# Transnormer attention with an RWKV channel mix on one core: the last tile's two parts stored by one DMA each, one middle tile's stores cut in four

## The chip, the core and the metric

The kernel runs on one core of one Trainium2 chip. The metric is device time in microseconds (us) of one execution. Before the change the median of three runs is 197.99 us (197.79 to 198.03).

The core has five engines that work side by side: TensorE (PE, matrix products into the PSUM memory; PEld is its loading of weights), VectorE (DVE), ScalarE (ACT), GpSimd (POOL) and SyncE (SP). Data moves between the chip's main memory (DRAM) and the on-chip memory SBUF (128 partitions) by DMA. A DMA is issued by an instruction on an engine's queue (here SP, ACT or POOL), carried out by some of the core's 16 DMA engines in packets, and reported by a semaphore.

## The reference

The attention part multiplies, for each of 8 batches and 8 heads, q by k-transposed-times-v, normalises each row of 64, and scales it. The channel mix then mixes each token with the one before it, and gates one product by another:

```python
kv = np.einsum('bhsd,bhse->bhde', k, v)
out = np.einsum('bhsd,bhde->bhse', q, kv)
out = out / np.sqrt(np.mean(out * out, axis=-1, keepdims=True) + 1e-06) * g_norm
x = out.transpose(0, 2, 1, 3).reshape(B, S, H * D)            # 8 x 576 x 512
xk = mu_k * x + (1.0 - mu_k) * x_prev                         # x_prev: one token earlier
xr = mu_r * x + (1.0 - mu_r) * x_prev
k = np.maximum(xk @ w_k, 0.0)                                 # 512 -> 1024
v = k * k @ w_v                                               # 1024 -> 512
r = 1.0 / (1.0 + np.exp(-(xr @ w_r)))
return r * v                                                  # 8 x 576 x 512, float32
```

## The kernel before

**Tiles.** A batch has 576 tokens. They are dealt out as 9 groups j of 64 rows: token number is p times 9 plus j, with p from 0 to 63. Two batches are taken together, which makes 18 groups of 64, or 9 tiles of two groups: a tile t fills the 128 partitions, group 2t in partitions 0 to 63 and group 2t + 1 in partitions 64 to 127. A tile is named by its batch and number, (7, 8) being the last.

**Order.** `ORDER`, at the head of the kernel, is a list of words written by hand; each word is one step, and each engine carries out its instructions in the order in which the words emit them. The words that matter here:

- `R.b.t`: the gate of a tile, four matrix products (L665) and a sigmoid on ScalarE (L668) into a tile `sig`.
- `V.b.t.part`: the product with `w_v`, eight matrix products (L675) into a PSUM tile of 128 by 512.
- `fin.b.t`: `finish`. VectorE multiplies the PSUM tile by `sig` into an SBUF tile `out` (L688), float32, 128 by 512, and two stores follow on SyncE's queue, one for each half of the partitions.
- `fip.b.t` and `sta.b.t`: the same in two words, the first half's store on SyncE's queue, the second half's later on ScalarE's.
- `L.0` and `L.1`: the last tile (7, 8), computed by `last_vv` in two parts of its columns: the wide part, columns 0 to 383, and then the narrow one, 384 to 511. Each part has eight matrix products (L683), one multiplication (L688) and two stores, the first half's on SyncE's queue and the second half's on ScalarE's.

The end of `ORDER` is

```
... fin.6.3 fin.7.4 R.7.8=1 V.7.5.0=5 V.7.5.1 fip.7.7 fip.7.5 sta.7.7 sta.7.5 L.0=3 L.1=0
```

and the tile (4, 3), which the change names, is finished at the end of the seventh of the list's eight periods, after (5, 4) and before (6, 2):

```
... fin.5.4 ... V.4.3.1 ks.6.5' fin.4.3          (next period:)  ... V.6.2.1 fin.6.2 ...
```

**Stores.** `store` (L698 is its `dma_start`) writes one half of a tile: 64 partitions of `out` go to 64 rows of the result. In DRAM, rows of one group lie 9 rows of 512 floats apart; the two groups of a tile are neighbours, one row apart, as long as they lie in one batch. The groups of the last tile are 7 and 8 of batch 7.

**Tiles' room.** `out` tiles take one of seven buffers in turn; a buffer is given back when the second half's store is emitted (`leave`), and the next multiplication into it waits until its stores have landed.

**The end.** When the last word has been emitted, the closing code (L836 in the profile) has SyncE wait for every semaphore that is still open, and a barrier of all engines follows.

The tiles' names in the profile, with a number: `out__3425` is tile (4, 3), `out__3527` tile (6, 2), `out__3698` tile (7, 5), `out__3712` the wide part of the last tile, `out__3725` its narrow part.

Of the kernel before, what the change touches and what calls it, by code (L numbers as in the profile page):

```python
# [117 lines left out]
def kernel(  # L118
# [13 lines left out]
    nc = tc.nc  # L132

    B, H, S, HD = q.shape
    C = H * HD
# [3 lines left out]
    G = 9  # L139
# [43 lines left out]
    for w, mu in enumerate((moe_mu_k, moe_mu_r)):  # L183
        nc.sync.dma_start(out=rows[4 * w:4 * w + 4, :], in_=mu.rearrange("(j p) -> j p", p=128))
    nc.sync.dma_start(out=rows[8:9, :].rearrange("o (e p) -> o e p", e=2),
                      in_=g_norm.rearrange("(o p) -> o p", o=1).unsqueeze(1).to_broadcast([1, 2, HD]))
# [58 lines left out]
    def take(key, shape, dtype, name):  # L245

        n = chosen.pop(0) if chosen else idle[0]
        idle.remove(n)
        held[key] = n, bank(n, shape, dtype, name)
        return held[key][1]  # L250

    def give(key):
        n, ps = held.pop(key)
        idle.append(n)
        return ps
# [13 lines left out]
    def half(i):  # L269
        return slice(64 * i, 64 * i + 64)  # L270
# [376 lines left out]
    def slot(kind, key, shape, dtype):  # L647

        n = place[kind, key] = free[kind].pop(0)
        return work.tile(shape, dtype, tag=f"{kind}{n}_", name=f"{kind}{n}_", bufs=1)  # L650

    def leave(kind, key):
        free[kind].append(place.pop((kind, key)))
# [24 lines left out]
    def last_vv(b, t, part):  # L678

        c = (slice(0, 3 * C // 4), slice(3 * C // 4, C))[part]  # L680
        ps = take(("last", part), [128, c.stop - c.start], FP32, "ps_v")
        for fc in range(NFC):
            nc.tensor.matmul(ps, sqk[:, fc, 128 * t:128 * t + 128], wv_sb[:, fc, c], start=(fc == 0), stop=(fc == NFC - 1))  # L683
        finish(b, t, ("last", part), c, (nc.sync, nc.scalar))

    def finish(b, t, key, c=slice(0, C), queues=(nc.sync, nc.sync)):
        o = outs[b, t, c.start] = slot("out", (b, t, c.start), [128, c.stop - c.start], FP32)
        DVE.tensor_mul(out=o, in0=give(key), in1=sig[b, t][:, c])  # L688
        for i, q_ in enumerate(queues):
            store(b, t, i, q_, c)  # L690
        if c.stop - c.start == C:
            leave("sig", (b, t))

    outs = {}

    def store(b, t, i, q_, c=slice(0, C)):
        bb, j = b - b % 2 + (2 * t + i) // G, (2 * t + i) % G
        q_.dma_start(out=out[bb].rearrange("(p j) c -> j p c", j=G)[j, :, c], in_=outs[b, t, c.start][half(i), :])  # L698
        if i == 1:
            leave("out", (b, t, c.start))  # L700

# [3 lines left out]
    for what in "wk.0.2 wk.1.2 k.0.2 q.0.2 v.0.2 wv.0.2 k.1.2 q.1.2 v.1.2 wv.2.4 wv.3.4 wr.0.1".split():  # L705
        name, i, n = what.split(".")
# [29 lines left out]
    def part_square(b, j, f0, f1, eng):  # L736
# [36 lines left out]
        "V": lambda eng, b, t, part: vv(b, t, part),  # L773
        "Vq": lambda eng, b, t, part: vv(b, t, part, 2),
        "fin": lambda eng, b, t: finish(b, t, ("v", b, t)),
        "fip": lambda eng, b, t: finish(b, t, ("v", b, t), queues=(nc.sync,)),
        "sta": lambda eng, b, t: store(b, t, 1, nc.scalar),
        "L": lambda eng, part: last_vv(B - 1, 8, part),
        "tab": lambda eng: ACT.preload_act_table_set("sigmoid_and_others"),  # L779
        "cast": lambda eng, n: evac(eng, x_in["kv"[n], 0][:, A], raw[:, n]),  # L780
# [60 lines left out]
```

## Time and profile before

| | |
|---|---|
| median of three runs | 197.99 us |
| the profiled execution | 198.81 us |
| its span, first to last instruction | 197.0 us |
| PE busy | 187.9 us, 95% of the span, mean granted clock 0.996 |
| DVE, ACT, POOL busy | 160.2, 135.3 and 28.2 us |
| DMA moved | 32.75 MB in 42958 packets |
| read and written in DRAM | 33.56 and 9.44 MB |

The profile belongs to one execution. Its span runs from the first instruction to the last; 1.81 us of that execution's time lie around it. An engine's busy time says how much of the span it worked. Instructions that issue a DMA are not counted as busy; they are listed for the queues SPq, ACTq and POOLq with the time that the issue took. What a DMA does after that is told by the DMA engines' share of busy time, by the bytes moved, by the count of packets, and by the time from issue to landing.

### The profile page before, as it was taken

Reading aid. Unit: us, or ns where it says so; the run is one execution under the profiler, and the core shown is the slowest. Engines: PE = TensorE matmul, PEld = TensorE weight load, DVE = VectorE, ACT = ScalarE, POOL = GpSimd, SP = SyncE. Lnnn points to the kernel's source line nnn. Section 1 sums busy time; section 2 is a strip of 40 time slices with the busy share of each in tenths; the row PEclk is TensorE's granted clock in tenths of the full one; section 3 lists DMA queues with packets and bytes.
Section 4 is the critical chain, followed back from the end, with each engine's and each line's share of the span. In section 5 each row is a group of like instructions: output and inputs, shape, how many; then the busy total and the mean of one; then the engine's idle time right before and its main releaser. Section 6 shows DMA issues by size and latency. Waiting matters only on the chain.

```text
span 197.0 us, 5692 instructions
## 1 busy us (share of the span) xinstructions
PE 187.9 (95%) x2343; PEld 110.3 (56%) x2343; DVE 160.2 (81%) x355; ACT 135.3 (69%) x273; POOL 28.2 (14%) x50
## 2 busy tenths in 40 slices
PE   7698999999999997999999999999999999999991
PEld 2345665465554774566744666765446666655441
DVE  1479899999999997999989999899998678465341
ACT  3494876765876995899594869998892867435520
POOL 7753334010023003200020040000000000000000
PEclk9999999999999999999999999999999999999998
DMA  5999999999999999999979889977526313125185
GB/s 216 215 211 206 194 207 209 206 207 241 257 200 149 216 265 128 221 230 246 200 121 173 163 149 245 229 104 104 142 53 118 86 43 77 25 57 131 40 210 152
DMA packets 42958, 32.75 MB, mean 166 GB/s; under 512 B 23852, under 2 KB 37428, under 8 KB 42932
## 3 DMA queue, kind: packets, MB, share of 16 engines
q0 software_dynamic: 14400, 16.19, 49.6%
q1 hardware_dynamic: 28132, 15.67, 36.7%
q10 hardware_dynamic: 400, 0.52, 0.9%
q8 instruction: 18, 0.29, 0.6%
q14 instruction: 8, 0.07, 0.1%
HBM read 33.56 MB, written 9.44 MB: 218 GB/s over the span
## 4 chain that ended last, share of the span: by engine, by line
PE 63%; DMA 24%; DVE 5%; POOL 2%; ACT 2%; issue 2%; DVEq 0%; POOLq 0%
PE ps_v L675 25%; PE ps_km L633 20%; PE ps_r L665 12%; DMA in_q<-in_q_dram 8%; DMA sq<-in_k_dram 7%; DMA qT__1367<-in_q 5%; DMA q<-in_q_dram 3%; PE ps_kv L287 2%; PE ps_u L317 1%; DVE yd L400 1%; PE ps_x L437 1%; DVE xr L620 1%; PE ps_v L683 1%; ACT L779 1%; DVE ss__2775 L362 1%
## 5 line engine op out<-in xcount | busy, mean ns | idle before, releaser
L675 PE MATMUL ps_v<-wv_sb,sqk 128*128 128x512 bf16 x280 | 66.6, 379 | 0.0
L633 PEld LDWEIGHTS <-wk_sb 128*128 128x128 bf16 x480 | 45.7, 98 | 17.0
L675 PEld LDWEIGHTS <-sqk 128*128 128x128 bf16 x280 | 26.6, 98 | 28.3 <-issue 0.2
L665 PE MATMUL ps_r<-wr_sb,xr 128*128 128x512 bf16 x144 | 34.8, 379 | 0.1
L665 PEld LDWEIGHTS <-xr 128*128 128x128 bf16 x144 | 14.0, 98 | 14.4 <-issue 0.3
L625 ACT ACTIVATE rt<-ps_km 128x320 bf16<-128x320 f32 (+2 forms) x17 | 7.9, 496 | 5.3 <-PE ps_km L633 3.5
L260 PE MATMUL ps_warm<-zeros 128*128 128x512 bf16 x28 | 9.2, 441 | 1.2 <-DVE eps L223 1.2
L633 PE MATMUL ps_km<-xk__880,wk_sb 128*128 128x192 bf16 (+1 forms) x64 | 9.2, 287 | 0.0
L633 PE MATMUL ps_km<-xk__3387,wk_sb 128*128 128x288 bf16 x64 | 9.0, 286 | 0.0
L633 PE MATMUL ps_km<-xk__2408,wk_sb 128*128 128x288 bf16 x64 | 8.7, 286 | 0.0
L633 PE MATMUL ps_km<-xk__1965,wk_sb 128*128 128x288 bf16 x64 | 8.7, 286 | 0.0
L633 PE MATMUL ps_km<-xk__2742,wk_sb 128*128 128x288 bf16 x64 | 8.7, 286 | 0.0
L633 PE MATMUL ps_km<-xk__3233,wk_sb 128*128 128x288 bf16 x64 | 8.7, 286 | 0.0
L633 PE MATMUL ps_km<-xk__1507,wk_sb 128*128 128x288 bf16 x64 | 8.3, 286 | 0.0
L427 ACT ACTIVATE xT<-ps_x,cols 128x256 bf16<-128x256 bf16 (+3 forms) x9 | 5.2, 588 | 3.6 <-PE ps_x L437 3.5
L260 PEld LDWEIGHTS <-zeros 128*128 128x128 bf16 x28 | 2.9, 109 | 5.0 <-issue 2.4
L724 PE MATMUL ps_km<-xk__371,wk_sb 128*128 128x320 bf16 x32 | 5.1, 300 | 0.5 <-DMA wk_sb<-in_moe_w_k_dram 0.5
L195 POOL DMA_DIRECT2D in_v<-in_v_dram x3 | 2.2, 747 | 19.7 <-PE ps_kv L287 17.2
L641 DVE TENSOR_TENSOR sqk<-rt 128x768 bf16<-128x768 bf16 (+3 forms) x7 | 4.9, 703 | 0.1
L427 ACT ACTIVATE xT<-xT,cols 128x1152 bf16<-128x1152 bf16 x4 | 5.0, 1294 | 0.0
L603 ACT ACTIVATE m__2401<-dx__2391,cols 128x576 bf16<-128x576 bf16 x4 | 2.9, 768 | 3.1 <-DVE dx__2391 L597 3.1
L688 DVE TENSOR_TENSOR out__3637<-ps_v,sig__3631 128x512 f32<-128x512 f32 x1 | 0.7, 691 | 5.3 <-ACT sig__3631 L668 5.3
(417 smaller groups left out, 372.7 us busy)
## 6 DMA issues: line engine op xcount, KB each, us to landing
q<-in_q_dram POOLq DMA_DIRECT2D x3, 576.0 KB, 14.7
sq<-in_k_dram POOLq DMA_DIRECT2D x3, 576.0 KB, 14.5
qT<-in_v_dram POOLq DMA_DIRECT2D x3, 576.0 KB, 11.4
in_v<-in_v_dram POOLq DMA_DIRECT2D x3, 576.0 KB, 14.7
in_q<-in_q_dram POOLq DMA_DIRECT2D x3, 576.0 KB, 10.2
in_k<-in_k_dram POOLq DMA_DIRECT2D x3, 576.0 KB, 17.0
wk_sb<-in_moe_w_k_dram POOLq DMA_DIRECT2D x2, 512.0 KB, 10.0
sqk<-in_k_dram SPq DMA_DIRECT2D x1, 576.0 KB, 3.7
```

The lines of the kernel that those rows point to most:

```text
L195: nc.gpsimd.dma_start(out=x_in[name, b], in_=by_token(dram[name], b))
L260: nc.tensor.matmul(ps, zeros[:, :128], zeros, start=True, stop=True)
L287: nc.tensor.matmul(ps[e][half(i), M, :], kb[half(e), 2 * M + i, tok(j)], vb[half(e), 2 * M + i, tok(j)], start=(j == 0), stop=(j == G - 1))
L317: nc.tensor.matmul(out_, qT_[half(r), b // 2, half(ct % 2)], kv_[half(r), 0 if r == i else 1, ct, :], start=True, stop=True)
L427: eng.activation(out=dst, in_=src, func=AF.Copy, scale=g_sb)
L603: eng.activation(out=out_, in_=in_, func=AF.Copy, scale=mu)
L625: eng.activation(out=dst, in_=ps, func=AF.Relu)
L633: nc.tensor.matmul(ps[:, n, :], wk_sb[:, cc, 128 * fc:128 * fc + 128], at[b]["xk"][:, cc, c0:c1], start=(cc == 0), stop=(cc == NHP - 1))
L641: eng.tensor_mul(out=sqk[:, fcs, o:o + n], in0=src, in1=src)
L665: nc.tensor.matmul(ps, xr[:, cc, 128 * t:128 * t + 128], wr_sb[:, cc, :], start=(cc == 0), stop=(cc == NHP - 1))
L675: nc.tensor.matmul(ps, sqk[:, fc, 128 * t:128 * t + 128], wv_sb[:, fc, :], start=(fc == 0), stop=(fc == NFC - 1))
L724: nc.tensor.matmul(ps[:, n, :], wk_sb[:, cc, 128 * fc:128 * fc + 128], at[0]["xk"][:, cc, c0:c1], start=(cc == 0), stop=(cc == NHP - 1))
```

## The change

`last_vv` no longer has `finish` store its parts. It issues one DMA for each part, over all 128 partitions: the wide part's on ScalarE's queue, the narrow part's on SyncE's. The DMA's DRAM side has three dimensions: 2 groups, 64 rows, the part's columns. Its SBUF side has two: 128 partitions, the part's columns. In the last tile two DMAs stand in place of four.

`finish` treats the tile (4, 3) apart: each of its two stores is cut into two halves of the columns, on the same queue, so that four DMAs of 64 rows and 256 columns stand in place of two of 64 rows and 512 columns. The address of a half's rows moves from `store` into a function of its own, `rows_of`.

```diff
@@ last_vv
-        finish(b, t, ("last", part), c, (nc.sync, nc.scalar))
+        finish(b, t, ("last", part), c, ())
+        (nc.scalar, nc.sync)[part].dma_start(
+            out=out[b].rearrange("(p j) c -> j p c", j=G)[2 * t - G:2 * t - G + 2, :, c], in_=outs[b, t, c.start])

@@ finish
         for i, q_ in enumerate(queues):
-            store(b, t, i, q_, c)
+            if (b, t) == (4, 3):
+                for c_ in (slice(0, C // 2), slice(C // 2, C)):
+                    q_.dma_start(out=rows_of(b, t, i)[:, c_], in_=outs[b, t, c.start][half(i), c_])
+                if i == 1:
+                    leave("out", (b, t, c.start))
+            else:
+                store(b, t, i, q_, c)

+    def rows_of(b, t, i):
+        bb, j = b - b % 2 + (2 * t + i) // G, (2 * t + i) % G
+        return out[bb].rearrange("(p j) c -> j p c", j=G)[j]
+
     def store(b, t, i, q_, c=slice(0, C)):
-        bb, j = b - b % 2 + (2 * t + i) // G, (2 * t + i) % G
-        q_.dma_start(out=out[bb].rearrange("(p j) c -> j p c", j=G)[j, :, c], in_=outs[b, t, c.start][half(i), :])
+        q_.dma_start(out=rows_of(b, t, i)[:, c], in_=outs[b, t, c.start][half(i), :])
```

## The prediction

> **What bounds the kernel now.** I read the engines' busy times first (PE 187.9 us of a span of 197.0, 95%), then the chain of waits, which says what ended last, then the instructions of the last microseconds in order of time, and last the DMA engines' share over short windows. The chain's last pieces (start, length, what):
>
> ```profile
> 189.61 1.73 PE ps_v L675 x8
> 191.34 1.31 PE ps_v L683 x8
> 192.66 0.04 DVEq L688
> 192.69 0.04 issue
> 192.74 0.06 DVE out__3712 L688
> ```
>
> PE never rests until 193.09, so whatever the change does before that is worth nothing unless it holds up PE. What remains is a tail of 3.9 us, from 193.1 to 197.0. The last instructions in order of time (start, length, queue, what):
>
> ```profile
> 192.74 0.56 DVE L688 TENSOR_TENSOR out__3712<-ps_v,sig__3684 128x384 f32<-128x384 f32 x1 [0.67 <-PE ps_v L683]
> 193.21 0.28 DVE L688 TENSOR_TENSOR out__3725<-ps_v,sig__3684 128x128 f32<-128x128 f32 x1
> 193.32 0.47 SPq L698 DMA_DIRECT2D out_dram<-out__3712  x1
> 193.32 0.50 ACTq L698 DMA_DIRECT2D out_dram<-out__3712  x1
> 193.88 0.55 SPq L698 DMA_DIRECT2D out_dram<-out__3725  x1
> 193.92 0.79 ACTq L698 DMA_DIRECT2D out_dram<-out__3725  x1
> ```
>
> The reader is to see that the narrow part is ready at 193.49 but its stores start only at 193.88 and 193.92, because each queue is still issuing its wide store. The DMA list gives 2.2 us from issue to landing for the last one, so it lands at 193.92 + 2.2 = 196.1, and the closing barrier takes the other 0.9 us. Now the DMA engines over short windows (window, its length, four columns of engine work, clock, then the DMA share and GB/s):
>
> ```profile
> 176.94:177.18 0.24, 0.24 (x3) 0.10 (x1) 0.24 (x1) 0.24 (x2) 0.00 (x0) 1.00 0.07 26
> ...
> 194.37:194.44 0.07, 0.00 (x0) 0.00 (x0) 0.00 (x0) 0.00 (x0) 0.00 (x0) 1.00 0.00 0
> 194.46:194.86 0.40, 0.00 (x0) 0.00 (x0) 0.00 (x0) 0.00 (x0) 0.00 (x0) 1.00 0.94 204
> 194.98:195.12 0.14, 0.00 (x0) 0.00 (x0) 0.00 (x0) 0.00 (x0) 0.00 (x0) 1.00 1.02 362
> ...
> 195.68:197.00 1.32, 0.00 (x0) 0.00 (x0) 0.00 (x0) 0.00 (x0) 0.00 (x0) 0.50 0.00 0
> ```
>
> Three things. The engines rest at 194.37 to 194.44 and start on the wide store at 194.46: 1.14 us after its issue, 0.09 us after the stores before it have ended. Then they are busy until 195.68, so the last two stores' bytes take **1.22 us**, and another 1.32 us pass between the last byte and the end of the span. And the first line is a single engine (a share of 0.07 is one of sixteen) that had fallen behind on a store: alone, it moves **26 GB/s**.
>
> **How many engines a DMA uses.** This decides the case. Each engine that takes part ends its share with one small packet, so the count of small packets tells how many took part. The DMA view of three windows, on SyncE's queue: one around the second load of `rows` (4 rows, L184), one around the load of `g_norm` (2 rows, L185), one around two ordinary stores of 64 rows:
>
> ```profile
> q1 hardware_dynamic: 8, 0.00, 5.5%
> ```
>
> ```profile
> q1 hardware_dynamic: 4, 0.00, 3.0%
> ```
>
> ```profile
> DMA packets 160, 0.26 MB, mean 164 GB/s; under 512 B 32, under 2 KB 32, under 8 KB 160
> ```
>
> 8 packets are 4 rows and 4 ends; 4 are 2 rows and 2 ends; 160 are 128 rows and 32 ends, 16 for each store. So a DMA whose outermost dimension counts 64 is dealt over 16 engines, one that counts 4 over 4, one that counts 2 over 2. The new stores have 128 rows, but the DRAM side's outermost dimension is the pair of groups: it counts **2**. My reading is that the outermost dimension is what is dealt out, and that each new store runs on two engines, 64 rows on each.
>
> The Trainium skill, "DMA: Bandwidth & Descriptors", section "Why a DMA increments its semaphore by 16 and not by 1", states it as a rule: the number of engines is the largest up to 16 that divides the slowest dimension of both sides, and on these queues they are the lowest-numbered ones. The three counts agree; no run here yet shows 128 against 2. By it the sum below stands with both stores on the same two engines.
>
> **The change part by part.**
>
> *Two stores fewer in the tail.* Gone are one issue on SP (0.47) and one on ACT (0.79). SP has then been free since 192.57, so the narrow store starts at 193.49 + 0.03 (the lag that the wide one shows: multiplication ends 193.30, issue 193.32) = 193.52, 0.4 us earlier. Nothing is queued behind either issue but the closing code. The wide store starts at 193.32 as before, from ACT. The 0.4 us are hidden: the narrow store's first byte could move 1.14 us later, at 194.66, and the engines that it needs are then in the wide one.
>
> *The bytes.* Wide 128 x 1536 = 196,608, narrow 128 x 512 = 65,536, together 262,144; on two engines 131,072 each. At 26 GB/s that is 5.04 us, the lower bound, since rows shorter than 2 KB can only be slower. For the upper bound of a busy engine I take the windows that hold only such rows: 362 GB/s at a share of 1.02 is 22 GB/s an engine, or 69 ns for 1536 B; 144 GB/s at a share of 0.60 (195.40 to 195.66) is 15 GB/s, or 34 ns for 512 B. 64 x (69 + 34) = 6.6 us. The second of these windows has pauses and end packets in it, so I take a value nearer the first bound, **5.5 us**. Whether the two stores alternate or follow each other doesn't matter to the sum.
>
> *The end.* 194.46 + 5.5 = 199.96, plus the 1.32 us from last byte to the end: 201.28, against 197.0: **+4.3 us**. The profiled execution goes from 198.81 to 203.1; it stands 0.82 above the median shown, so the median goes to 197.99 + 4.3 = 202.3. With the bounds of the bytes it is 201.8 to 203.4.
>
> *The middle tile.* (4, 3) is `out__3425`. Its two issues fill 165.70 to 166.81 on SP; two more of about 0.55 us each take SP to 167.9. SP's next issue is at 174.11, after a wait of 7.2 us for VectorE, which hides them: cost 0. Were that cover gone, the store of (6, 2) would be issued 1.1 us later; what is late then is only the return of an `out` buffer, of which there are seven. The bytes are the same and every store still has 64 rows in its outermost dimension. Nothing of PE's waits there, and with one SP store pair in 8 us the DMA engines have room for the shorter rows.
>
> **The rivals.**
>
> *Faster: all sixteen engines and both halves of the partitions at once.* If 128 rows are dealt over sixteen engines, the stores gain. A half tile alone goes at 204 GB/s, the second half after it at 362: in the profile a store of 64 partitions that starts on resting engines never gets past some 220. One store over 128 partitions would run at about 362 from the start: 0.54 us for the wide part, 0.3 for the narrow one (64 KB at 204 GB/s), so the bytes end at 195.30 in place of 195.68, and the time is 197.6. Against it: the outer count of 2, and the counts of ends above. It decides from nine engines up: at 24 GB/s each they would move the 262,144 bytes in the present 1.22 us. The Trainium skill, "SBUF — State Buffer", section "Door 1: The DMA port swizzle", would have it so: partitions 0 to 63 reach only half of the DMA ports, and one transfer over all 128 is advised. The 204 beside the 362 agrees with it. I give 0.10.
>
> *No change: sixteen engines, but the wide store alone at 204 GB/s.* 0.96 us and 0.3 for the narrow one are 1.26, as before: 198.0. 0.05.
>
> *Two engines each, but not the same two.* Then the wide store alone decides: 98,304 B an engine, at 24 GB/s 4.1 us; 194.46 + 4.1 + 1.32 = 199.9, +2.9 us: 200.9. Nothing in the profile says which engines a short DMA takes. 0.08.
>
> *Two engines at the slow rate.* The 204 GB/s of the first half are 13 GB/s an engine. If that is what one queue gives to an engine, and not two engines in each other's way, the bytes take 10.1 us and the time is 206.9. The single engine's 26 speaks against it. 0.04.
>
> **How the numbers follow.** The forecast, both stores on the same two engines, has 0.73. The predicted time is its 202.3. The range goes down to 200.6, to take in the rival of different engines, and up to 204.6, beyond the bound of 203.4 by the pauses that a queue of 64 rows on one engine may have. It leaves out the two rivals on sixteen engines (0.15 together) and the slow rate (0.04). 0.2%, or 0.4 us, is about what a measurement of this kernel can tell from no change. Slower by more than that: 0.73 + 0.08 + 0.04 = 0.85. The faster rival's 0.4 us lies at that bound; I put most of it beyond, 0.08, and the rest with the no-change rival, 0.07.
>
> **What would show it.** Right: the two last stores with 128 rows and 4 end packets in all (2 each), a DMA share of about 0.12 (2 of 16) and some 50 GB/s from 194.5 to about 200, a time to landing of over 5 us for at least one of them, and a span near 201.3 with PE's work up to 193.1 unchanged. The narrow store's issue at 193.52, and four issues from 165.70 to about 167.9 on SP with (6, 2) still at 174.1, would show the two small steps. Wrong: 16 end packets from each store and a DMA share near 1 that ends before 195.7, which is the faster rival; a share of 0.25 would be two pairs of engines. If PE's last product moved from 193.1, the middle tile would not have been free.

## The result and the profile after

The changed kernel takes 203.58 us (median of six runs, 202.76 to 204.08) against 198.17 us for the kernel before (six runs, 197.79 to 199.04): a ratio of 1.0263, 95% interval 1.0231 to 1.0296. It is slower by 5.4 us. The profiled execution takes 202.76 us and has a span of 201.0 us, 4.0 more than before's. Its last 9 us, in order of time:

```profile
191.53 0.56 DVE L690 TENSOR_TENSOR out__3714<-ps_v,sig__3686 128x384 f32<-128x384 f32 x1 [0.67 <-PE ps_v L683]
192.01 0.28 DVE L690 TENSOR_TENSOR out__3726<-ps_v,sig__3686 128x128 f32<-128x128 f32 x1
192.12 1.07 ACTq L685 DMA_DIRECT2D out_dram<-out__3714  x1
192.31 0.56 SPq L685 DMA_DIRECT2D out_dram<-out__3726  x1
```

TensorE's chain ends 1.2 us earlier than in before's profile. That is not the change: in the profiles of the experiments below the same multiplication starts anywhere between 191.4 and 193.6. So the two kernels are compared by their **tail**, from the start of the wide part's multiplication to the end of the span: 4.31 us before (192.735 to 197.042), 9.44 after (191.533 to 200.972), 5.1 more. The DMA engines in that tail (window, length, four columns of engine work, clock, DMA share, GB/s):

```profile
193.18:193.34 0.16, 0.00 (x0) 0.00 (x0) 0.00 (x0) 0.00 (x0) 0.00 (x0) 1.00 0.00 0
193.36:195.70 2.34, 0.00 (x0) 0.00 (x0) 0.00 (x0) 0.00 (x0) 0.00 (x0) 1.00 0.13 31
195.80:199.10 3.30, 0.00 (x0) 0.00 (x0) 0.00 (x0) 0.00 (x0) 0.00 (x0) 0.61 0.14 48
199.25:199.65 0.40, 0.00 (x0) 0.00 (x0) 0.00 (x0) 0.00 (x0) 0.00 (x0) 0.50 0.14 44
199.75:201.00 1.25, 0.00 (x0) 0.00 (x0) 0.00 (x0) 0.00 (x0) 0.00 (x0) 0.50 0.00 0
```

A share of 0.13 is two of sixteen engines, for 6.4 us. The DMA view of the same stretch, with what was moved in 40 slices:

```profile
GB/s 27 18 27 9 46 36 46 9 27 46 18 55 55 18 15 49 49 49 49 49 49 49 49 49 49 49 49 49 49 49 49 39 49 49 49 43 42 46 9 0
DMA packets 260, 0.26 MB, mean 39 GB/s; under 512 B 4, under 2 KB 260, under 8 KB 260
...
q10 hardware_dynamic: 130, 0.20, 9.4%
q1 hardware_dynamic: 130, 0.07, 3.2%
```

130 packets on each queue are 128 rows and **2** end packets. The strip shows two phases: pauses for the first 2.4 us, when only the wide store's rows move, then a steady 49 GB/s, when wide and narrow rows alternate on the same two engines. (A pause is no idle engine in this trace: the share is 0.13 in both phases, and the packet records of the first have rows of 126 to 300 ns among rows of 65.) And SyncE around tile (4, 3), which is `out__3425` here too:

```profile
160.14 1.11 SPq L709 DMA_DIRECT2D out_dram<-out__3383  x2
164.50 2.38 SPq L694 DMA_DIRECT2D out_dram<-out__3425  x4
172.91 1.11 SPq L709 DMA_DIRECT2D out_dram<-out__3529  x2
```

Four issues end at 166.88; the next is 6 us later, after a wait for VectorE.

### The profile page after: what moved, and what is told of

It is laid out like the page before. It is cut to its first block, busy times and chain, and to the rows that moved or that the text cites. A ratio compares the mean times of both kernels' runs of the same rounds, so it can differ in the third digit from the quotient of the medians.

```text
span 201.0 us, 5691 instructions
## 1 busy us (share of the span) xinstructions
PE 188.8 (94%) x2343; PEld 110.6 (55%) x2343; DVE 160.2 (80%) x355; ACT 135.4 (67%) x273; POOL 28.1 (14%) x50
## 3 DMA queue, kind: packets, MB, share of 16 engines
HBM read 33.56 MB, written 9.44 MB: 214 GB/s over the span
## 4 chain that ended last, share of the span: by engine, by line
PE 79%; DMA 5%; DVE 5%; POOL 3%; ACT 2%; issue 2%; DVEq 0%; POOLq 0%
PE ps_v L675 28%; PE ps_km L633 26%; PE ps_r L665 15%; DMA wk_sb<-in_moe_w_k_dram 5%; PE ps_kv L287 2%; PE ps_u L317 2%; PE ps_km L735 1%; PE ps_x L437 1%; DVE yd L400 1%; POOL rt L182 1%; PE ps_qt L331 1%; POOL q L182 1%; PE ps_warm L260 1%; DVE xr L620 1%; PE ps_v L683 1%
## 5 line engine op out<-in xcount | busy, mean ns | idle before, releaser
L260 PE MATMUL ps_warm<-zeros 128*128 128x512 bf16 x28 | 9.8, 468 | 1.2 <-DVE eps L223 1.2
```

The costliest lines, as they stand in the source:

```text
L260: nc.tensor.matmul(ps, zeros[:, :128], zeros, start=True, stop=True)
```

## The experiments

Eleven kernels ran, in three groups; each group's runs stand beside runs of the kernel before on the same chip, whose medians are 198.44 us (`last_only` to `paired_halves`), 198.64 (`rows_62` to `paired_full`) and 198.22 (the last three). Tails and their parts are read from the profiles, the parts from the DMA packets: from the start of the wide multiplication to the first byte, the bytes, and from the last byte to the end of the span. They come from one profile of each kernel. Where two kernels store the last tile alike, these readings agree closely: the bytes of the change and `last_only` within 0.03 us, of before and `mid_only` within 0.01.

| run | time, us | ratio to before (95%) | tail | to first byte | bytes | to the end |
|---|---|---|---|---|---|---|
| before | | | 4.31 | 1.71 | 1.23 | 1.37 |
| the change | 203.58 | 1.0263 (1.0231 to 1.0296) | 9.44 | 1.82 | 6.37 | 1.25 |
| last_only | 203.48 | 1.0262 (1.0225 to 1.0299) | 9.51 | 1.82 | 6.34 | 1.35 |
| mid_only | 198.35 | 1.0008 (0.9986 to 1.0030) | 4.67 | 1.72 | 1.22 | 1.74 |
| paired_one | 198.28 | 0.9991 (0.9960 to 1.0022) | 4.02 | 1.86 | 0.88 | 1.28 |
| paired_halves | 198.49 | 1.0006 (0.9981 to 1.0031) | 4.42 | 1.82 | 1.23 | 1.37 |
| rows_62 | 203.60 | 1.0253 (1.0203 to 1.0302) | 9.69 | 1.58 | 6.81 | 1.30 |
| rows_63 | 199.14 | 1.0030 (0.9997 to 1.0062) | 4.94 | 1.52 | 1.91 | 1.51 |
| narrow_one | 199.94 | 1.0052 (1.0017 to 1.0087) | 5.47 | 1.71 | 2.44 | 1.31 |
| paired_full | 198.30 | 0.9983 (0.9950 to 1.0016) | 4.00 | 1.85 | 0.89 | 1.26 |
| wide_one | 202.17 | 1.0191 (1.0138 to 1.0243) | 8.26 | 1.82 | 5.06 | 1.37 |
| one_queue | 203.86 | 1.0274 (1.0229 to 1.0320) | 9.53 | 1.79 | 6.50 | 1.24 |
| halves_queues | 198.74 | 1.0011 (0.9978 to 1.0045) | 4.42 | 1.73 | 1.40 | 1.29 |

**The change's two halves apart.** In `last_only`, `last_vv` is as in the change and `finish` as before; in `mid_only` the other way round.

> Only the last tile's part of the change; tile (4, 3) is stored as before. The tail is counted from the start of the wide part's multiplication to the end of the span: 4.3 us before, 9.5 us after. Theory (a store whose DRAM side has 2 as its outermost dimension runs on two DMA engines, and nothing else costs anything): a tail of 9.5 us, the time within 0.4 us of the whole change, some 203.6, 2 end packets from each of the two stores. Rival (the middle tile's four stores hold something up as well): faster than the whole change by more than 0.4 us.

> Only the middle tile's part of the change: (4, 3) stored in four, the last tile as before. Theory: no difference that can be measured, 198.2 with a ratio to before between 0.998 and 1.002, a tail of 4.3 us, four issues of about 0.55 us each on SP and (6, 2)'s store not later. Rival (the four stores cost part of the 5.4 us): a ratio above 1.003.

The last tile's part makes the whole loss: a ratio of 1.0262 for the change's 1.0263. The middle tile's part makes nothing that the times can tell, but its tail was expected at 4.3 us and is 4.67. Two lines of SyncE's waits in the closing code, first before, then `mid_only` (what it waits for: total, times, longest):

```profile
SPq L836 <- DMA out_dram<-out__3712: 0.9, 1, 0.9
...
SPq L836 <- DMA out_dram<-out__3725: 0.2, 1, 0.2
```

```profile
SPq L845 <- DMA out_dram<-out__3727: 1.6, 1, 1.6
```

In the closing code SyncE waits for one semaphore after the other, in a fixed order. Before, it comes to the wide stores' semaphores first and to the narrow ones' last. In `mid_only`, where two DMAs more have been issued, the narrow stores have got the semaphores that are waited for first, so that SyncE stands at them for 1.6 us and goes through all the others, long since reached, only after the last byte has landed: 1.74 us from last byte to end in place of 1.37. With the whole change two DMAs more and two fewer cancel out: 1.25, against 1.35 in `last_only`. So by these profiles the middle tile saves the change 0.1 us of its tail, which is too little for the times to tell.

**Which dimension is dealt out.** `paired_one` is the change with the DRAM side turned round, 64 rows outermost and the 2 groups inside. The rows of the last tile come out in another order; bytes, row lengths, queues and DMAs are the same.

```diff
-            out=out[b].rearrange("(p j) c -> j p c", j=G)[2 * t - G:2 * t - G + 2, :, c], in_=outs[b, t, c.start])
+            out=out[b].rearrange("(p j) c -> p j c", j=G)[:, 2 * t - G:2 * t - G + 2, c], in_=outs[b, t, c.start])
```

> The whole change, but with the DRAM side of the two last stores given as 64 rows outermost and the 2 groups inside; the SBUF side stays 128 partitions, so that the result's rows of the last tile come out in another order. Queues, bytes, row lengths and the number of DMAs are those of the change. Theory (the outermost dimension is dealt over the engines): 16 end packets from each store, the tail falls from 9.5 to about 3.9 us, 0.4 below before, since one store over 128 partitions moves at about 360 GB/s from its start; time about 197.8. Rival 1 (one queue, or one DMA of 128 rows, is slow by itself): tail stays near 9.5 us, time near 203.5. Rival 2 (sixteen engines, but no gain from 128 partitions): tail 4.2 to 4.4 us, time 198.2.

One line's order of dimensions takes the tail from 9.44 to 4.02 us. The DMA view of its last two stores:

```profile
DMA packets 288, 0.26 MB, mean 226 GB/s; under 512 B 32, under 2 KB 288, under 8 KB 288
```

and two windows, the first with wide rows alone:

```profile
193.50:193.80 0.30, 0.00 (x0) 0.00 (x0) 0.00 (x0) 0.00 (x0) 0.00 (x0) 1.00 1.03 379
...
194.34:195.60 1.26, 0.00 (x0) 0.00 (x0) 0.00 (x0) 0.00 (x0) 0.00 (x0) 1.00 0.00 0
```

32 end packets, 16 for each store, where the change had 2; and 379 GB/s, where before's wide store, half the partitions at a time, began at 204. Neither a queue nor a DMA of 128 rows is slow by itself.

`paired_halves` keeps before's four stores and turns only their order of rows in the same way (32 rows outermost, 2 groups inside):

```diff
-        finish(b, t, ("last", part), c, (nc.sync, nc.scalar))
+        finish(b, t, ("last", part), c, ())
+        for i, q_ in enumerate((nc.sync, nc.scalar)):
+            q_.dma_start(out=out[b].rearrange("(p j) c -> p j c", j=G)[32 * i:32 * i + 32, 2 * t - G:2 * t - G + 2, c],
+                         in_=outs[b, t, c.start][half(i), :])
```

> Before, with the last tile's four stores kept (64 partitions each, SP and ACT), but each with the DRAM side of 32 rows outermost and the 2 groups inside; the rows of the last tile come out in another order. It is the same order of rows in DRAM as in the run with 64 outermost, at before's number of DMAs. Theory: 16 end packets from each store, tail 4.3 us and time as before, 198.2; so that the difference to the run with 64 outermost is what one store over 128 partitions brings in place of two over 64 each, 0.4 us. Rival (neighbouring rows written by one DMA are slow, or fast, by themselves): a tail off by more than 0.3 us from 4.3.

Its bytes take 1.23 us, as before. So of the 0.35 us between 1.23 and `paired_one`'s 0.88 nothing comes from the order of rows in DRAM; it is what one store over 128 partitions brings in place of two over 64.

**By divisors.** `rows_62` and `rows_63` keep before's four stores and cut each from 64 rows to 62 or 63; the rest of the rows is not stored.

```diff
...
+            q_.dma_start(out=out[b].rearrange("(p j) c -> j p c", j=G)[2 * t - G + i, :62, c],
+                         in_=outs[b, t, c.start][64 * i:64 * i + 62, :])
```

> Before, with each of the last tile's four stores cut from 64 rows to 62, so that two rows of each of its groups are not stored; no dimension of 2 anywhere, 3% fewer bytes, queues and number of DMAs as before. Theory (a DMA is dealt over the largest number of engines up to 16 that divides its outermost count): 62 = 2 x 31, so each store runs on 2 engines and leaves 2 end packets, all four on the same two; each engine has 62 wide and 62 narrow rows, tail about 9.3 us and time about 203.3, as slow as the change. Rival (the pair of groups in one DMA is what is slow, or 128 rows in one DMA): tail 4.3 us and time as before, 198.4.

> The same with 63 rows in place of 64, one row of each group not stored. Theory: 9 is the largest divisor of 63 up to 16, so 9 end packets from each store and 7 rows of it on each engine; 28 rows an engine in place of 16, at 61 and 23 ns 1.2 us, in place of the present 1.2 us which the half-partition rate sets: tail 4.3 to 4.9 us, time 198.4 to 199.0. Rival (only powers of two are dealt, an odd count runs on one engine): over 10 us of bytes, tail above 13 us.

The DMA views from shortly after the first row on, when only these stores are left, first 62, then 63 rows:

```profile
DMA packets 250, 0.24 MB, mean 35 GB/s; under 512 B 8, under 2 KB 250, under 8 KB 250
```

```profile
DMA packets 262, 0.22 MB, mean 118 GB/s; under 512 B 36, under 2 KB 262, under 8 KB 262
```

8 ends are 2 for each of four stores; 36 are 9 for each. Two rows fewer than 64 make the tail 5.4 us longer, with no pair of groups anywhere; one row fewer makes it 0.6 longer, which the times can't yet tell from nothing (1.0030, interval from 0.9997). With 63 rows the bytes take 1.91 us where 1.2 were expected. Two windows show where some of that went:

```profile
194.06:195.00 0.94, 0.00 (x0) 0.00 (x0) 0.00 (x0) 0.00 (x0) 0.00 (x0) 1.00 0.51 153
...
195.50:195.95 0.45, 0.00 (x0) 0.00 (x0) 0.00 (x0) 0.00 (x0) 0.00 (x0) 1.00 0.20 57
```

Nine engines at full work are a share of 0.56. At first they are nearly all busy, but at 153 GB/s they move some 19 GB/s each, where a 1536 B row in 61 ns is 25; in the last 0.45 us most of them have ended already. Why the rows are slower here is open.

**Each store by itself.** In `narrow_one` only the narrow part is stored as in the change, in `wide_one` only the wide one; the other keeps its two halves.

> Only the narrow part stored by one DMA on SP as in the change; the wide part by two stores as before; (4, 3) as before. Theory: the narrow store's 64 rows on each of two engines cost 64 x 23 ns = 1.5 us behind the wide stores' 8 rows of 1536 B, so the last byte comes about 1.0 to 1.3 us later than before: tail 5.3 to 5.6 us, time about 199.5. Rival (what slows the change is the descriptors' making, not the bytes): a tail of 6.5 us or more.

> Only the wide part stored by one DMA on ACT as in the change, the narrow part by two stores of 64 rows as before. In the change the bytes took 6.37 us where 64 x (61 + 23) ns are 5.4; the wide store's first 24 rows on each engine took 2.4 us, with pauses, before the narrow store's first row. Theory A (the pauses belong to the making of the wide store's own rows, 64 for each of two engines): the pauses stay, 64 wide rows take 3.9 + 0.9 = 4.8 us, and the narrow stores' 8 rows on those two engines add 0.2: bytes 5.0 us, tail 8.0 us, time about 202.1. Theory B (the pauses come from the narrow store's rows being made for the same two engines meanwhile): few pauses, bytes 4.1 us, tail 7.2 us, time about 201.3.

In the bytes' time the two stores add up: the narrow one alone adds 1.21 us and the wide one alone 3.83, together 5.04, where the change adds 5.14. The narrow store's 1.21 is 64 rows on each of two engines at 23 ns, less what before took for it. A window of it:

```profile
196.15:197.70 1.55, 0.00 (x0) 0.00 (x0) 0.00 (x0) 0.00 (x0) 0.00 (x0) 1.00 0.14 42
```

Two engines again, 42 GB/s, and no pauses. The wide store alone takes 5.06 us of bytes where 4.8 to 5.0 were worked out with pauses and 4.1 without: the pauses are the wide store's own. A line of its DMA list shows a further cost:

```profile
out_dram<-out__3724 ACTq DMA_DIRECT2D x1, 32.0 KB, 5.5
```

The narrow part's second half, a sixteen-engine store of 32 KB behind the wide one on ScalarE's queue, takes 5.5 us to land, since two of its engines still carry the wide store.

**Queues.** `one_queue` is the change with both stores on SyncE's queue; `halves_queues` has the change's queues without its merging, both wide halves on ScalarE's and both narrow halves on SyncE's.

> The change with both of the last stores on SP's queue, wide first. Theory (the same two engines, the sum of the rows doesn't depend on their order or queue): the narrow rows follow the wide ones and don't alternate with them, bytes 6.0 to 6.6 us with theory A, 5.4 to 5.6 with theory B, tail 9.1 to 9.7 or 8.6; time 203.2 or 202.7. Rival (ACT's queue, whose issue of the wide store took 1.07 us, is what makes the pauses): bytes 5.4 us, with no pauses though the wide rows are made alone.

> The change's queues without its merging: both halves of the wide part on ACT's queue, both halves of the narrow part on SP's, 64 rows each; (4, 3) as before. Theory: 16 end packets from each of four stores; the second wide store is issued 0.55 us later than before, at the time at which the first one's bytes end, so bytes 1.2 to 1.5 us, tail 4.3 to 4.6, time as before, 198.6. Rival (the choice of queues costs something by itself): tail above 5 us.

On one queue the narrow rows follow the wide ones instead of alternating. The wide rows' first and second stretch, and the narrow rows:

```profile
194.46:196.90 2.44, 0.00 (x0) 0.00 (x0) 0.00 (x0) 0.00 (x0) 0.00 (x0) 0.79 0.13 30
196.94:199.39 2.45, 0.00 (x0) 0.00 (x0) 0.00 (x0) 0.00 (x0) 0.00 (x0) 0.50 0.13 50
199.45:200.90 1.45, 0.00 (x0) 0.00 (x0) 0.00 (x0) 0.00 (x0) 0.00 (x0) 0.50 0.14 43
```

The sum hardly moves, 6.50 for 6.37, and the slow first 2.4 us are there on SyncE's queue too, so ScalarE's longer issue (1.07 us) is not their cause. The queues alone cost nothing that the times can tell: 4.42 us of tail in `halves_queues`, a ratio of 1.0011.

`halves_queues` shows one thing more. Its two wide halves follow each other on ScalarE's queue; a window in the first, and one in the second:

```profile
194.05:194.45 0.40, 0.00 (x0) 0.00 (x0) 0.00 (x0) 0.00 (x0) 0.00 (x0) 1.00 0.88 207
194.80:195.10 0.30, 0.00 (x0) 0.00 (x0) 0.00 (x0) 0.00 (x0) 0.00 (x0) 1.00 1.02 230
```

On one queue both halves are slow. In before, where the second half was issued at the same time as the first but on the other queue, the second moved at 362 GB/s (194.98 to 195.12), though it too is a store of 64 partitions.

**A version on sixteen engines with the right rows.** `paired_full` stores as `paired_one` does, and reorders the last tile's tokens to fit: for batch 7, `add` writes the last 128 columns of `xk` and `xr` in the order row, group. All that follows works token by token and is left as it is.

```diff
...
+        z = S - 2 * P
+        DVE.tensor_add(out=dst[:, :, :z], in0=m[:, hs, :z], in1=x[:, hs, :z])
+        DVE.tensor_add(out=dst[:, :, z:].rearrange("q h (p j) -> q h j p", j=2),
+                       in0=m[:, hs, z:].rearrange("q h (j p) -> q h j p", j=2),
+                       in1=x[:, hs, z:S].rearrange("q h (j p) -> q h j p", j=2))
```

> The change with 64 rows outermost and the 2 groups inside on the DRAM side, and the tokens of the last tile reordered to fit: the adds for batch 7 write the last 128 columns of xk and xr in the order of row, group (two adds in place of one, four adds more on VectorE in all). Theory: the last tile's stores run on 16 engines over 128 partitions as in the run with the rows in another order, tail 4.0 us, and the four adds hide under TensorE's work, so the time is 0.3 us under before, ratio 0.9985. Rival (the adds hold up the products of batch 7): TensorE's last product 0.3 us or more later, ratio 1.000 or above.

Its tail is 4.00 us, 0.31 under before's, and its median lies 0.3 us under before's, a ratio of 0.9983. The interval, 0.9950 to 1.0016, holds 1, so the tail shows the gain and the time doesn't yet. One of the four adds of batch 7, now in two parts, the second of them reordered:

```profile
160.96 0.63 DVE L624 TENSOR_TENSOR xk__3387<-m__3358,xT 128x896 bf16<-128x896 bf16 x1 [0.95 <-ACT m__3358 L603]
161.62 0.45 DVE L625 TENSOR_TENSOR xk__3387<-m__3358,xT 128x256 bf16<-128x256 bf16 x1
```

The pair takes 1.11 us where one add took some 0.75; TensorE shows no idle time in any 5 us window from 160 to 190.

## Why the prediction was right, and where it was off

**The mechanism held.** The forecast's reading, that the outermost dimension is dealt out and that a DRAM side beginning with 2 leaves two engines, came from two small loads and two ordinary stores. (The load that it calls 2 rows reads one row twice: its outermost dimension is 1, and the 2 comes next; the count of 2 engines holds for it.) The change's own 2 end packets for each store, the 16 of `paired_one` and the 2 and 9 of `rows_62` and `rows_63` show it, and show that it is divisors that count: 62 runs on 2, 63 on 9. The Trainium skill, "DMA: Bandwidth & Descriptors", section "Why a DMA increments its semaphore by 16 and not by 1", gives just that rule, the largest number up to 16 that divides the slowest dimension of both sides; the trace agrees for 128 against 2, 62 and 63.

**The size: the bytes.** Predicted +4.3 us; the tails say +5.1 and the medians +5.4. The term that was sized too small is "The bytes", for which I took 5.5 us; it measured 6.37, inside its bound of 6.6. The whole 5.1 us of the tail is in this term, 6.37 for 1.23; the tail's other two parts moved by 0.1 each, one up and one down. The steady rate was right: 64 pairs of a wide and a narrow row at 85 ns are 5.4 us. What the 5.5 left out is the pauses of the wide store's first 24 rows on each engine, 2.4 us in place of 1.5; the forecast had named such pauses, without a size, as a reason for the upper end of its range alone. `wide_one` and `one_queue` show that they belong to the wide store, whatever its queue and without the narrow store on two engines; what makes them is not settled. The other terms: first byte 1.24 us after the wide issue where 1.14 was taken, last byte to end 1.25 where 1.32 was. The remaining 0.3 us between tails and medians is within the scatter of the runs.

**The narrow store's start.** It was issued 0.19 us after the wide one, as predicted, and the gain was hidden, as predicted; but its first row moved 3.43 us after its issue, not 1.14, and only then did the two stores alternate. For the sum it made no difference, as `one_queue` shows.

**The same two engines.** The rival of different engines falls: with both stores in flight the share is 0.14, which is two engines and not four, and wide and narrow rows alternate at 49 GB/s, twice one engine's 26 less the short rows' cost.

**The faster rival was a right account of another kernel.** It put one store over 128 partitions on sixteen engines at 197.6; `paired_one` measured a tail 0.29 us shorter, where the working gave 0.38, and a ratio of 0.9991 whose interval (0.9960 to 1.0022) holds 1. The Trainium skill, "SBUF — State Buffer", section "Door 1: The DMA port swizzle", has 64 partitions reach half the ports; 379 GB/s for `paired_one`'s wide rows beside 204 for before's first half agrees. Before's second half does not: 362 GB/s from 64 partitions is far above half of 379. So the prediction's line that the 204 beside the 362 agrees with the rule doesn't hold, since both are stores of 64 partitions. That one store over 128 partitions is faster is shown, and why is open. In the change itself nothing of it could show, since only two engines asked.

**The middle tile.** Its cost was 0, as said: SyncE's next store came 6 us later. That it could gain some 0.1 us at the closing waits, by moving the semaphores on by two, was not foreseen.

## What to carry to other kernels

Before merging stores, look at the outermost dimension of both sides of the DMA (in these runs the DRAM side or both had the awkward count, never the SBUF side alone): it is what is dealt over the engines, by divisors, and a 2 in front, or 62 rows in place of 64, turns sixteen engines into two. Count the end packets of a short stretch to see how many took part. A store over all 128 partitions is worth having when the count stays at 16 (0.3 us of the tail here), and near the end of a kernel the order in which the closing code waits for semaphores is worth 0.1 to 0.4 us of the tail.

## What the runs showed of the hardware that was not expected

A store of 64 rows of 1536 B on each of two engines begins with pauses: its first 24 rows an engine took 2.4 us, 100 ns a row, against 61 ns later (`one_queue`). Rows of 512 B on two engines, issued while sixteen engines were busy, showed none (42 GB/s throughout). A half tile of wide rows behind the other half moved at 362 GB/s when it stood on the other queue (before), and at 230 behind it on the same queue (`halves_queues`). And a store on sixteen engines can be held to 5.5 us by two of them, when another store on its queue has loaded those two.
